# Moving the second weight conversion and the next step's weight sums later in layer 1's first product

## The chip, the cores and the metric

The kernel runs on one core of one Trainium2 chip. The metric is the device time of one execution in microseconds (us). The kernel before takes 1036.18 us (median of 3 runs, 1035.57 to 1036.93). One further execution was profiled; its trace is what all rows below come from.

## The reference

An attention with a sigmoid in place of the softmax is followed by two layers of two matrix products each. Only the first product of the first layer (`x @ w_in`) is touched here.

```python
def _attn_ref(q, k, v):            # 4 x 12 heads, 448 x 64
    scores = scale * q @ k.T - log(S)
    return (1 / (1 + exp(-scores))) @ v

def _moe_ref(x, w_in, w_out):      # x 1792 x 768, w_in 768 x 2048
    h = x @ w_in
    g = h * (1 / (1 + exp(-h)))
    return g @ w_out

def _moe2_ref(x, w_in, w_out, a, b):
    h = x @ w_in
    g = P(h) / (Q(h) + 1e-6)       # a cubic over a quadratic
    return g @ w_out
```

The inputs q, k, v and the weights arrive as float64 and the kernel turns them into float32 itself.

## The kernel before, in words

Every float32 operand of a matmul is split into a high part (a copy cast by ScalarE) and a low part (source minus high part, by VectorE); a product is then three matmuls: high with high, low with high, high with low. Layer 1's first product is done by a seven-product scheme on halves of the matrices: each of the 16 steps g of the loop at L1183 makes seven products p1 to p7, each of nine matmuls of 128x448, with weights that are halves of w_in's blocks and sums of them. A step covers two blocks of 128 of the hidden width for one of two halves of the batch (t = 0 for g below HF = 8, then t = 1).

TensorE's order within step g is p1(g), p2(g), p4(g-1), p6(g), p5(g), p3(g-1), p7(g). Each of the five engines has its own queue of instructions, and the code is written in the very order in which they are put there; nothing reorders it.

The names in the rows, which leave out buffer numbers:

- `wf` holds the float32 weights of a step, two tiles (first and second half) for even and two for odd steps. For g up to 7 they come from a conversion; for later ones from DRAM (`load_w1`, L588).
- A conversion (`conv`, L209) makes a float32 tile from the bits of a float64 one: two ScalarE instructions (L226, L227), then two VectorE instructions (L228, L229). The second half of step g+1's weights is converted in step g after p2 (for g from 1 to 6); the first half of step g+2's at the end of step g, after p7 (for g up to 5). A DMA writes the result to DRAM and another loads the next float64 tile (`conv_outs`, L180).
- `sf` holds four sums: S1 and S2 (`sums_12`, L602: VectorE L448 with `sf<-wf`, then L445 with `sf<-sf,wf`) and S3 and S4 (`sums_34`, L612: two times L445).
- `wr` and `wq` are the split weights. `prep_ij` casts the first half (wr0, `wr<-wf`), `prep_s12` casts S1 and S2 (wr2, `wr<-sf`), `prep_s3` and `prep_s4` cast S3 (wq0) and S4 (wq2, both `wq<-sf`), `prep_a22` casts a quarter (wq4, `wq<-wf`). The casts are ScalarE's L436; the low parts wr1, wr3, wq1, wq3, wq5 are VectorE's L441, issued by the next `flush`.
- p1 and p2 use wr0 and wr1, p6 and p5 use wr2 and wr3, p7 uses wq0 and wq1, p3 uses wq2 and wq3, p4 uses wq4 and wq5.
- `keep` (ScalarE L649) copies a bank of products out, `both` (VectorE L448 with `sb<-acc` or `sb<-hb`) adds another bank to it, and the `silu` calls c11, c12, c21, c22 (ScalarE L593) make the result and have it stored. c21 reads its bank directly.
- `fill` and `operands1` prepare the second half's x operands in steps 1, 3 and 5 (ScalarE L426, VectorE L427 and L445), two operands in each.

The banks of products are the two halves of one tile `hb` (L1046) and six tiles `acc`. The first bank list of `bank` (L565) gives p1, p4, p6 and p7 of a step one bank, the last gives p5 and p3 one: with g mod 3 = 1 the former is hb's first half, with g mod 3 = 2 the latter is hb's second half.

Of the kernel before, what the change touches and what calls it, by code (L numbers as in the profile page):

```python
# [47 lines left out]
def attention_moe_moe(ctx: ExitStack, tc: tile.TileContext, q, k, v, w_in1, w_out1, w_in2, w_out2, a, b2, out):  # L48
# [12 lines left out]
    HF = KF // 2  # L61
# [11 lines left out]
    def fixed(nm, n, shape, dt, pool=cpool):  # L73
        return [pool.tile(shape, dt, tag=f"{nm}{i}", name=f"{nm}{i}") for i in range(n)]
# [105 lines left out]
    def conv_outs():  # L180
        for do in outs:
            do()
        outs.clear()
# [25 lines left out]
    def conv(parted=False, into=None):  # L209
        i = done["conv"]  # L210
        if i >= len(order):
            return
        m, kind, c = order[i]
        t = staged.pop(i)
        lo, hi = t[:, :, 0], t[:, :, 1]
        u = bits.get() if into is None else into
        ui = u.bitcast(I32)
        if into is not None:
            kept_by = partial(conv_kept, wd[m][c][kind], u, t)
        elif (m, kind) == (0, "o") and c >= direct[0]:  # L220
            kept_by = partial(conv_split, c, u, t)
        else:
            kept_by = partial(conv_out, wd[m][c][kind], u, t)
        done["conv"] += 1
        if not parted:
            nc.scalar.activation(u, hi.bitcast(F32), AF.Prelu, scale=DOWN, alpha=NEGATIVE)  # L226
            nc.scalar.activation(lo, t.bitcast(U16)[:, :, 1], AF.Identity, bias=mid, scale=EIGHTH)  # L227
            nc.vector.tensor_scalar(u, u, MOST_DOWN, -MOST_DOWN * NEGATIVE, op0=ALU.min, op1=ALU.max)  # L228
            nc.vector.scalar_tensor_tensor(  # L229
                out=ui, in0=ui, scalar=3, in1=lo, op0=ALU.logical_shift_left, op1=ALU.bitwise_or  # L230
            )
            outs.append(kept_by)
            return
        nc.scalar.activation(u, hi.bitcast(F32), AF.Abs)
        nc.vector.tensor_scalar(u, u, LEAST, MOST, op0=ALU.max, op1=ALU.min)
        nc.vector.tensor_scalar(ui, ui, 3, REST, op0=ALU.logical_shift_left, op1=ALU.bitwise_and)

        def rest():
            nc.vector.scalar_tensor_tensor(
                out=ui, in0=hi, scalar=SIGN_TOP, in1=ui, op0=ALU.bitwise_and, op1=ALU.bitwise_or  # L240
            )
            nc.vector.scalar_tensor_tensor(
                out=ui, in0=lo, scalar=29, in1=ui, op0=ALU.logical_shift_right, op1=ALU.bitwise_or
            )
            outs.append(kept_by)

        halves.append(rest)
# [77 lines left out]
    wf = [fixed(f"wf{i}_", 2, [P, DM], F32, w1_p) for i in range(2)]  # L325
# [109 lines left out]
    def split_later(src, h, lo):  # L435
        nc.scalar.copy(h, src)  # L436
        lows.append((src, h, lo))

    def flush():
        for src, h, lo in lows:  # L440
            nc.vector.tensor_tensor(out=lo, in0=src, in1=h.bitcast(F32), op=ALU.subtract)  # L441
        lows.clear()

    def sub(o, i0, i1):
        nc.vector.tensor_tensor(out=o, in0=i0, in1=i1, op=ALU.subtract)  # L445

    def add(o, i0, i1):
        nc.vector.tensor_tensor(out=o, in0=i0, in1=i1, op=ALU.add)  # L448
# [84 lines left out]
    def operands1_late(kind):  # L533
        temps = [t[:, :S] for t in xio.free]
        if kind == "T2":
            for kk in range(HK):
                load_b(temps[kk], 1, 0, kk, 1)
        if kind in ("T2", "T1"):
            for kk in range(HK):
                split_b(kept[kind, kk], 1, kind, kk)  # L540
        if kind == "T1":
            for kk in range(HK):
                load_b(kept["T1", kk], 1, 1, kk, 1)
        if kind == "T3 sums":
            for kk in range(HK):
                sub(temps[kk], kept["T1", kk], temps[kk])
        if kind == "T3":
            for kk in range(HK):
                split_b(temps[kk], 1, kind, kk)
            for kk in range(HK):  # L550
                load_b(temps[kk], 1, 1, kk, 0)
        if kind == "22":
            for kk in range(HK):
                split_b(kept["T1", kk], 1, kind, kk)
        if kind == "T4 sums":
            for kk in range(HK):
                sub(temps[kk], temps[kk], kept["T2", kk])
        if kind == "T4":
            for kk in range(HK):
                split_b(temps[kk], 1, kind, kk)  # L560
# [41 lines left out]
    def sums_12(g):  # L602
        if g < NGR:
            t, u = wf[g % 2]
            add(s12f[:, :HM], u[:, :HM], u[:, HM:])
            sub(s12f[:, HM:], s12f[:, :HM], t[:, :HM])
# [10 lines left out]
    def prep_s3(g):  # L617
        split_later(s34f[:, :HM], wq[0], wq[1])
# [7 lines left out]
    def p1(g):  # L626
        product(g, "11", bank("a", g), wr[0], wr[1], 0, True)

    def p2(g):
        product(g, "21", bank("b", g), wr[0], wr[1], HM, True)  # L630
# [4 lines left out]
    def p4(g):  # L635
        product(g, "T4", bank("a", g), wq[4], wq[5], 0, False)
# [10 lines left out]
    def keep(g, nm):  # L647
        t = sums[g, nm] = f448.get()
        nc.scalar.copy(t, bank("a", g))  # L649

    def both(g, nm, kind):
        t = sums[g, nm]
        add(t, bank(kind, g), t)
# [4 lines left out]
    def c12(g):  # L658
        silu(sums[g, "r"], sums[g, "r"], g, 0, 1)
# [381 lines left out]
    with tc.manual_schedule():  # L1041
# [141 lines left out]
        for g in range(NGR):  # L1183
            was = g >= 1

            p1(g)
            flush()
            if was:
                keep(g - 1, "u3")
            if g >= 2:  # L1190
                c12(g - 2)
            if g == HF:
                operands1_late("T3")
            if g == HF + 1:
                operands1_late("22")

            p2(g)
            flush()
            keep(g, "s1")
            if was:  # L1200
                both(g - 1, "u3", "c")
            conv_outs()
            if 1 <= g < HF - 1:
                conv(into=wf[(g + 1) % 2][1])
            sums_34(g)
            if g == HF - 1:
                operands1_late("T2")

            if was:
                p4(g - 1)  # L1210
                c22(g - 1)
            flush()
            both(g, "s1", "b")
            sums_12(g + 1)
            if was:
                fill(g)
            if g > HF:
                conv()
            if g == last - 3:
                third[0] = stage3  # L1220

            p6(g)
            flush()
            c11(g)
            if was:
                c21(g - 1)
            prep_s3(g)
            if g == HF - 1:
                operands1_late("T1")
            if g == HF:  # L1230
                operands1_late("T4 sums")
            if g == last:
                once.extend([*xio.free, *(xp[4][:, j].bitcast(F32) for j in range(2))])
                fg.put(*once)
                for n in range(5):
                    load_g(n)

            p5(g)
            flush()
            keep(g, "r")  # L1240
            conv_outs()
            prep_ij(g + 1)
            if g:
                prep_a22(g)
            fill(g)
            if g == HF:
                operands1_late("T4")
            if g == last:
                split_wo1(0)
                split_gd(0)  # L1250

            if was:
                p3(g - 1)
            flush()
            if g + 2 >= HF:
                load_w1(g + 2)
            conv_outs()
            if g == last:
                both(g - 1, "r", "c")
            if g == HF - 1:  # L1260
                operands1_late("T3 sums")
            if g == last - 1:
                kt_s.close()
                wos_p, wos_s = opened("wos", side="right")
                wos.put(*fixed("wos", 4, [P, DM], F32, wos_p))
                for c in range(4):
                    load_wo1(c)
            if g == last:
                split_wo1(1)
                split_gd(1)  # L1270
                load_wo1(4)

            p7(g)
            flush()
            if was and g < last:
                both(g - 1, "r", "c")
            prep_s12(g + 1)
            prep_s4(g)
            if g < HF - 2:
                conv(into=wf[g % 2][0])  # L1280
            elif g in (HF + 2, HF + 4):
                conv()
# [127 lines left out]
        for n in range(HN):  # L1410
            g, p = turn(n)
# [118 lines left out]
```

## Time and profile before

| what | value |
|---|---|
| median of 3 runs | 1036.18 us |
| the profiled execution | 1036.96 us |
| its span, first to last instruction | 1035.2 us |
| TensorE busy | 1025.6 us (99%) |
| VectorE busy | 690.2 us (67%) |
| ScalarE busy | 654.8 us (63%) |
| layer 1's first product | from 158.8 us to about 360 us |

Busy time counts matmuls whose ends are modelled, so that a small pause of TensorE is best seen at its weight loads (PEld), which run one ahead of the matmuls. The waits are inferred from semaphore events. Where an engine waits for several, the one that came last by the profile is named.

### The profile page before, as it was taken

Reading aid. Unit: us, or ns where it says so; the run is one execution under the profiler, and the core shown is the slowest. Engines: PE = TensorE matmul, PEld = TensorE weight load, DVE = VectorE, ACT = ScalarE, POOL = GpSimd, SP = SyncE. Lnnn points to the kernel's source line nnn. Section 1 sums busy time; section 2 is a strip of 40 time slices with the busy share of each in tenths; the row PEclk is TensorE's granted clock in tenths of the full one; section 3 lists DMA queues with packets and bytes.
Section 4 is the critical chain, followed back from the end, with each engine's and each line's share of the span. In section 5 each row is a group of like instructions: output and inputs, shape, how many; then the busy total and the mean of one; then the engine's idle time right before and its main releaser. Section 6 shows DMA issues by size and latency. Waiting matters only on the chain.

```text
span 1035.2 us, 15920 instructions
## 1 busy us (share of the span) xinstructions
PE 1025.6 (99%) x5568; PEld 894.3 (86%) x5568; DVE 690.2 (67%) x982; ACT 654.8 (63%) x971; POOL 270.2 (26%) x242
## 2 busy tenths in 40 slices
PE   9999999999999999999999999999999999999998
PEld 6555558889999988999998888888999999999998
DVE  4567756888977656354545538889897967555761
ACT  6788877777776666364645568676778866444430
POOL 4335420000000000000000065878959922310000
PEclk9999999999999999999999999999999999999999
DMA  8967856887786766598979634665778879986641
GB/s 173 211 147 169 190 148 207 283 294 261 231 291 245 263 245 209 189 385 273 398 277 406 252 109 157 213 226 201 261 254 312 273 230 295 321 282 204 218 157 54
DMA packets 182352, 246.15 MB, mean 238 GB/s; under 512 B 57152, under 2 KB 136640, under 8 KB 182272
## 3 DMA queue, kind: packets, MB, share of 16 engines
q1 hardware_dynamic: 168352, 220.95, 65.5%
q10 hardware_dynamic: 11152, 17.36, 4.8%
q0 software_dynamic: 2768, 6.82, 2.6%
q8 instruction: 44, 0.72, 0.3%
q14 instruction: 36, 0.29, 0.1%
HBM read 161.45 MB, written 83.62 MB: 237 GB/s over the span
## 4 chain that ended last, share of the span: by engine, by line
PE 69%; DVE 8%; ACT 2%; DMA 1%; issue 1%; SPq 0%; DVEq 0%; ACTq 0%
PE hp L996 12%; PE acc L574 11%; PE acc L722 6%; PE acc L721 6%; PE acc L723 6%; PE hp L794 5%; PE hp L795 5%; PE hp L796 5%; PE hb L996 4%; PE hb L574 4%; PE hb L722 2%; PE hb L723 2%; PE hb L721 2%; DVE sb L827 1%; DVE sb L825 1%; DVE sb L840 1%
## 5 line engine op out<-in xcount | busy, mean ns | idle before, releaser
L394 ACT ACTIVATE sb<-pair,nls 128x896 f32<-128x896 f32 x84 | 80.5, 1009 | 22.3 <-PE pair L379 22.3
L721 PE MATMUL acc<-xa_all,woH 128*128 128x512 f32 (+1 forms) x252 | 91.9, 365 | 0.0
L722 PE MATMUL acc<-xa_all,woH 128*128 128x512 f32 (+1 forms) x252 | 91.9, 365 | 0.0
L723 PE MATMUL acc<-xa_all,woL 128*128 128x512 f32 (+1 forms) x252 | 91.9, 365 | 0.0
L431 POOL TENSOR_TENSOR woL<-wif,woH 128x768 fp32r<-128x768 f32 x9 | 16.5, 1854 | 248.1 <-ACT woH L430 248.1
L823 POOL TENSOR_TENSOR sb<-sb 128x1024 f32<-128x1024 f32 (+1 forms) x32 | 69.3, 2166 | 39.4 <-ACT sb L820 39.4
L403 PE MATMUL hb<-sb,vs 128*64 128x448 f32 (+1 forms) x384 | 73.0, 554 | 0.0
L574 PE MATMUL acc<-xb,wr 128*128 128x448 f32 x315 | 66.9, 362 | 0.0
L226 ACT ACTIVATE sb<-sb 128x768 f32<-128x768 f32 x46 | 41.3, 898 | 40.1 <-DMA w1i<-sb 22.0
L914 POOL TENSOR_TENSOR sb<-sb 128x384 f32<-128x384 f32 (+1 forms) x43 | 52.2, 1220 | 53.9 <-DMA sb<-gk 51.9
L574 PEld LDWEIGHTS acc<-xb,wr 128*128 128x128 f32 x315 | 59.0, 187 | 4.6 <-issue 0.7
L796 PE MATMUL hp<-hx,woL 128*128 128x512 f32 (+1 forms) x168 | 60.7, 362 | 0.0
L794 PE MATMUL hp<-hx,woH 128*128 128x512 f32 (+1 forms) x168 | 60.7, 362 | 0.0
L795 PE MATMUL hp<-hx,woH 128*128 128x512 f32 (+1 forms) x168 | 60.7, 362 | 0.0
L794 PE MATMUL hp<-xa_all,woH 128*128 128x512 f32 (+1 forms) x168 | 60.7, 362 | 0.0
L795 PE MATMUL hp<-xa_all,woH 128*128 128x512 f32 (+1 forms) x168 | 60.7, 362 | 0.0
L796 PE MATMUL hp<-xa_all,woL 128*128 128x512 f32 (+1 forms) x168 | 60.7, 362 | 0.0
L820 ACT ACTIVATE sb<-sb,absb 128x1024 f32<-128x1024 f32 (+1 forms) x32 | 36.5, 1139 | 33.7 <-DVE hb L841 33.2
L228 DVE TENSOR_SCALAR sb<-sb 128x768 f32<-128x768 f32 x48 | 26.8, 558 | 41.7 <-ACT sb L226 41.5
L227 ACT ACTIVATE sb<-sb,ab 128x768 int32<-128x768 uint16 x54 | 53.6, 992 | 0.0
L825 DVE TENSOR_TENSOR sb<-hp,sb 128x768 f32<-128x768 f32 (+1 forms) x31 | 33.6, 1084 | 28.4 <-ACT sb L822 27.3
L229 DVE SCALAR_TENSOR_TENSOR sb<-sb 128x768 int32<-128x768 int32 x46 | 44.1, 959 | 12.2 <-ACT sb L227 10.8
(259 smaller groups left out, 2787.1 us busy)
## 6 DMA issues: line engine op xcount, KB each, us to landing
sb<-in_moe_w_out_dram SPq DMA_DIRECT2D x30, 768.0 KB, 6.7
sb<-in_moe_w_in_dram SPq DMA_DIRECT2D x28, 768.0 KB, 7.0
gd<-sb SPq DMA_DIRECT2D x64, 224.0 KB, 2.3
gk<-sb SPq DMA_DIRECT2D x28, 384.0 KB, 3.9
wf<-w0i SPq DMA_DIRECT2D x20, 384.0 KB, 5.4
gk<-sb SPq DMA_DIRECT2D x15, 512.0 KB, 3.0
woL<-gk SPq DMA_DIRECT2D x25, 256.0 KB, 5.0
w1i<-sb SPq DMA_DIRECT2D x16, 384.0 KB, 5.0
```

The source lines that it names most:

```text
L227: nc.scalar.activation(lo, t.bitcast(U16)[:, :, 1], AF.Identity, bias=mid, scale=EIGHTH)
L394: nc.scalar.activation(t, p[:, :, :S], AF.Sigmoid, bias=nls, scale=QKSCALE)
L403: nc.tensor.matmul(hb[i_ % 2][j * D : (j + 1) * D, :S], vs[i_][part, j, c * D : (c + 1) * D], t[part, j], start=(c == 0), stop=(c == LAST),)
L574: nc.tensor.matmul(o, w_[:, w], x[:, i_, :], start=first and kk == 0 and n_ == 0, stop=kk == HK - 1 and n_ == 2, skip_group_check=not first,)
L721: nc.tensor.matmul(o, woH[c][:, w], x[:, 0, :w_], start=(c == 0), stop=False)
L722: nc.tensor.matmul(o, woH[c][:, w], x[:, 1, :w_], start=False, stop=False)
L723: nc.tensor.matmul(o, woL[c][:, w], x[:, 0, :w_], start=False, stop=(c == KF - 1))
L794: nc.tensor.matmul(o, wh[:, w], x[:, 0, :wd_], start=first, stop=False)
L795: nc.tensor.matmul(o, wh[:, w], x[:, 1, :wd_], start=False, stop=False)
L796: nc.tensor.matmul(o, wl[:, w], x[:, 0, :wd_], start=False, stop=last)
L823: nc.gpsimd.tensor_tensor(out=q_, in0=q_, in1=a_, op=ALU.mult)
L996: nc.tensor.matmul(o, a_, y[:, w_, :], start=kk_ == 0 and n_ == 0, stop=kk_ == HF - 1 and n_ == 2)
```

## The change

The second conversion of a step goes from behind p2 to behind p6: in the code two products later, behind the calls c11, c21 and `prep_s3`. Its DMAs follow one call of `conv_outs` later. S1 and S2 of the next step's weights go from behind p4 to behind p3, three products later, into the queue behind the low parts of wr0 and wq4.

```diff
             conv_outs()
-            if 1 <= g < HF - 1:
-                conv(into=wf[(g + 1) % 2][1])
             sums_34(g)
...
             both(g, "s1", "b")
-            sums_12(g + 1)
             if was:
                 fill(g)
...
                 c21(g - 1)
             prep_s3(g)
+            if 1 <= g < HF - 1:
+                conv(into=wf[(g + 1) % 2][1])
...
             keep(g, "r")
-            conv_outs()
             prep_ij(g + 1)
...
             conv_outs()
+            sums_12(g + 1)
             if g == last:
                 both(g - 1, "r", "c")
```

On VectorE, in step 3 from behind p2 on (the row L448 with `sb<-hb` is `both` of u3, the one with `sb<-acc` that of s1; `sf_216` is S3 and S4, `sf_215` S1 and S2):

```order
 L448 TENSOR_TENSOR sb<-hb,sb 128x448
-L228 TENSOR_SCALAR wf_1_212<-wf_1_212 128x768
-L229 SCALAR_TENSOR_TENSOR wf_1_212<-wf_1_212,stage_1835 128x768
 L445 TENSOR_TENSOR sf_216<-wf_0_213,wf_1_214 128x384
 L445 TENSOR_TENSOR sf_216<-wf_0_213,sf_215 128x384
 L448 TENSOR_TENSOR sb<-acc_1852,sb 128x448
-L448 TENSOR_TENSOR sf_215<-wf_1_212 128x384
-L445 TENSOR_TENSOR sf_215<-sf_215,wf_0_211 128x384
 L427 TENSOR_TENSOR xa_all<-T_1841,xa_all 128x448
+L228 TENSOR_SCALAR wf_1_212<-wf_1_212 128x768
+L229 SCALAR_TENSOR_TENSOR wf_1_212<-wf_1_212,stage_1835 128x768
 L441 TENSOR_TENSOR wq_1724<-sf_216,wq_1723 128x384
```

The conversion's two instructions stand behind `both` of s1 now, ahead of wq1's low part, and S1 and S2 are gone from here.

On VectorE a few rows on in the same step, behind p3 (the last row is `both` of r, which reads hb's second half):

```order
 L441 TENSOR_TENSOR wr_1720<-wf_0_211,wr_1719 128x768
 L441 TENSOR_TENSOR wq_1728<-wf_1_214,wq_1727 128x384
+L448 TENSOR_TENSOR sf_215<-wf_1_212 128x384
+L445 TENSOR_TENSOR sf_215<-sf_215,wf_0_211 128x384
 L448 TENSOR_TENSOR sb<-hb,sb 128x448
```

S1 and S2 stand behind the low parts of wr0 and wq4, and `both` of r behind them.

On ScalarE in step 3 (L593 are c22, c11 and, with `sb<-acc`, c21; `wq_1723` is the cast of S3):

```order
 L649 COPY sb<-acc_1849 128x448
+L593 ACTIVATE sb<-sb 128x448
+L426 CAST xa_all<-T_1841 128x448
+L593 ACTIVATE sb<-sb 128x448
+L593 ACTIVATE sb<-acc_1850 128x448
+L436 CAST wq_1723<-sf_216 128x384
 L226 ACTIVATE wf_1_212<-stage_1835 128x768
 L227 ACTIVATE stage_1835<-stage_1835,ab 128x768
-L593 ACTIVATE sb<-sb 128x448
-L426 CAST xa_all<-T_1841 128x448
-L593 ACTIVATE sb<-sb 128x448
```

The conversion's two instructions stand behind c11, c21 and S3's cast. The cast of S1 and S2 (`wr<-sf`) keeps its place in ScalarE's queue, and so does everything behind it.

## Rows read from the trace of the kernel before

**Rows 1.** The page: the whole span, and TensorE's granted clock in 40 slices.

```profile
span 1035.2 us, 15920 instructions
PEclk9999999999999999999999999999999999999999
```

**Rows 2.** Timeline of weight loads: start, us, line, out<-in, count [idle before, releaser].

```profile
188.91 1.70 PEld L574 LDWEIGHTS hb<-xb,wr 128*128 128x128 f32 x9 [1.44 <-ACT sb L593]
...
207.78 1.71 PEld L574 LDWEIGHTS hb<-xb,wr 128*128 128x128 f32 x9 [0.97 <-ACT sb L227]
...
228.29 1.70 PEld L574 LDWEIGHTS hb<-xb,wr 128*128 128x128 f32 x9 [0.80 <-ACT sb L593]
...
246.21 1.79 PEld L574 LDWEIGHTS hb<-xb,wr 128*128 128x128 f32 x9
...
258.81 3.59 PEld L574 LDWEIGHTS acc<-xa_all,wr 128*128 128x128 f32 x18
...
266.32 1.71 PEld L574 LDWEIGHTS hb<-xb,wr 128*128 128x128 f32 x9 [0.32 <-ACT sb L593]
```

**Rows 3.** Timeline of VectorE, step 2 behind p2.

```profile
185.38 0.96 DVE L229 SCALAR_TENSOR_TENSOR wf<-wf,sb 128x768 int32<-128x768 int32 x1
186.26 0.55 DVE L445 TENSOR_TENSOR sf<-wf,wf 128x384 f32<-128x384 f32 x1
186.72 0.55 DVE L445 TENSOR_TENSOR sf<-wf,sf 128x384 f32<-128x384 f32 x1
187.19 0.62 DVE L448 TENSOR_TENSOR sb<-acc,sb 128x448 f32<-128x448 f32 x1
187.73 0.55 DVE L448 TENSOR_TENSOR sf<-wf 128x384 f32<-128x384 f32 x1
188.31 0.56 DVE L445 TENSOR_TENSOR sf<-sf,wf 128x384 f32<-128x384 f32 x1
```

**Rows 4.** Timeline of ScalarE, steps 2 and 3.

```profile
187.85 0.58 ACT L593 ACTIVATE sb<-sb 128x448 f32<-128x448 f32 x1 [2.41 <-DVE sb L448]
188.33 0.53 ACT L593 ACTIVATE sb<-hb 128x448 f32<-128x448 f32 x1
188.75 0.50 ACT L436 CAST wq<-sf 128x384 fp32r<-128x384 f32 x1
...
193.09 0.89 ACT L226 ACTIVATE wf<-sb 128x768 f32<-128x768 f32 x1
193.89 1.00 ACT L227 ACTIVATE sb<-sb,ab 128x768 int32<-128x768 uint16 x1
```

**Rows 5.** Timeline of VectorE, step 0: the low part of step 1's wr0.

```profile
165.78 0.96 DVE L441 TENSOR_TENSOR wr<-wf,wr 128x768 fp32r<-128x768 f32 x1 [0.79 <-ACT wr L436]
```

**Rows 6.** Timeline of ScalarE, step 3 behind p6.

```profile
202.46 0.53 ACT L649 COPY sb<-acc 128x448 f32<-128x448 f32 x1
202.88 0.84 ACT L436 CAST wr<-wf 128x768 fp32r<-128x768 f32 x1
203.62 0.52 ACT L436 CAST wq<-wf 128x384 fp32r<-128x384 f32 x1
204.03 0.57 ACT L426 CAST xa_all<-sb 128x448 fp32r<-128x448 f32 x1
204.50 0.84 ACT L436 CAST wr<-sf 128x768 fp32r<-128x768 f32 x1
```

**Rows 7.** Timeline of VectorE, step 3 behind p5.

```profile
204.64 0.63 DVE L427 TENSOR_TENSOR xa_all<-sb,xa_all 128x448 fp32r<-128x448 f32 x1 [1.46 <-ACT xa_all L426]
205.18 0.62 DVE L445 TENSOR_TENSOR T<-sb,T 128x448 f32<-128x448 f32 x1
205.71 0.95 DVE L441 TENSOR_TENSOR wr<-wf,wr 128x768 fp32r<-128x768 f32 x1
206.58 0.55 DVE L441 TENSOR_TENSOR wq<-wf,wq 128x384 fp32r<-128x384 f32 x1
207.05 0.62 DVE L448 TENSOR_TENSOR sb<-hb,sb 128x448 f32<-128x448 f32 x1
```

## The prediction, made before the changed kernel was run

> **What bounds the kernel now.** I read the page first, then TensorE's weight loads through layer 1's first product, then VectorE and ScalarE around each pause. TensorE is the bound: it hardly ever stops, and its clock is granted in full in all 40 slices [rows 1]. A step's seven products run unbroken in 258.81 - 246.21 = 12.60 us, 1.80 each [rows 2]. The first product shows only four pauses, 1.44, 0.97, 0.80 and 0.32, together 3.53 us [rows 2]; all end at a product whose bank is a half of hb. p5(2) begins at 188.91, 0.05 after c21 of step 1 ended (188.33 + 0.53 = 188.86) [rows 2, 4]. c21 read hb's first half while p5(2) writes the second, so I take it that hb is watched as one tile. p1(4), at 207.78, goes the same way: not ScalarE's L227, which the row names, but `both` of r (207.05 + 0.62 = 207.67) released it, 0.11 before [rows 2, 7]. So what TensorE waits for is how late VectorE and ScalarE are, and these two hand a step's work to and fro.
>
> **The change, part by part.** No instruction is added or removed, so only waits can change; each move is priced by who then waits.
>
> The conversion leaves VectorE's queue ahead of S3, S4 and `both` of s1. In step 2 its L229 alone holds 186.26 - 185.38 = 0.88, and c11 had ScalarE idle for 2.41 us until `both` of s1 was done [rows 3, 4]. That is a gain for c11 and c21, and with it for p5(2) and p5(5), if nothing else moves: 1.44 + 0.80 = 2.24 us [rows 2]. The DMAs behind it start later by at most a product or two and feed the third conversion on, a step and a half or 18.9 us later, so I price them at nothing; that cover fails if a load lands only after that.
>
> S1 and S2 are what decides. ScalarE's cast of them (wr2) keeps its place in the queue. In step 3 it starts at 204.50 [rows 6]. In the new order VectorE comes to S1 only behind the low part of wq4: 206.58 + 0.47 = 207.05, and then takes 188.31 - 187.73 = 0.58 for S1 and 0.56 for S2 [rows 3, 7]. That is 208.19, 3.69 us after the cast's turn, with nothing else late. Behind this cast in ScalarE's queue stand S4's cast, the next conversion and the `keep` of u3; behind these in VectorE's the conversion's other part, `both` of u3, S3, S4 and `both` of s1; then c11, c21, S3's cast and the second conversion back on ScalarE; then VectorE again up to the next S2. So the steps are now tied to one ring through both engines. I sum it from start to start of rows of the same form, the last of each stretch in full, 0.04 for a handoff (187.19 + 0.62 = 187.81 to 187.85) [rows 3, 4]:
>
> - ScalarE: wr2 0.74, S4's cast 0.41, L226 0.80, L227 1.00 = 2.95 [rows 4, 6].
> - VectorE: handoff 0.04, L229 0.88, the low parts of wr2 0.87 and of S4 0.47, `both` of u3 0.54, S3 0.46, S4 0.47, `both` of s1 0.62 = 4.35 [rows 3, 7].
> - ScalarE: handoff 0.04, c11 0.48, c21 0.42, S3's cast 0.41, L226 0.80, L227 1.00 = 3.15 [rows 4, 6].
> - VectorE: handoff 0.04, L229 0.88, low parts of S3 0.47, wr0 0.87, wq4 0.47, then S1 0.58 and S2 0.56 = 3.87, and a handoff of 0.04 back [rows 3, 7].
>
> A round is 14.36 us in an even step. In steps 1, 3 and 5 x operands are prepared too. From L227's end VectorE then waits for the second operand's cast, behind `keep` 0.42, wr0 0.74, wq4 0.41 and L426 0.57, less the 0.09 by which ScalarE takes its next instruction before L227 ends (an estimate from the overlaps of these rows), plus 0.04: 2.09 where an even step has 0.04 + 0.88 + 0.47 = 1.39. Then L427 takes 0.54 and L445 0.53 [rows 6, 7]. That adds 0.70 + 1.07 = 1.77: 16.13. TensorE needs 12.60, so it is not the one to close the ring.
>
> Where the ring begins: step 1's S1 now follows the low part of wr0, which starts at 165.78 [rows 5]: 165.78 + 0.87 + 0.58 + 0.56 = 167.79. Six steps (1 to 6) have the second conversion, three odd and three even: 3 x (14.36 + 16.13) = 91.47, so that step 7's S2 ends at 259.26. Behind it comes `both` of r, which starts 0.09 before that end (0.56 less the 0.47 between starts) and takes 0.62, and p1(7), on hb, waits for it with the 0.11 seen at p1(4): 259.26 - 0.09 + 0.62 + 0.11 = 259.90. Before, p1(7) began at 246.21 [rows 2]. Layer 1 is **13.7 us late** there, with the old pauses ahead of it contained.
>
> From step 7 on there is no second conversion, and the ring is open. What remains is S1 and S2, 0.58 + 0.47 = 1.05 us, ahead of `both` of r and late for the wr2 cast. Five more products write hb behind a read of it (p1(10), p1(13), p5(8), p5(11), p5(14)): the bounds are 0 and 5 x 1.05 = 5.3 us. Carrying the starts on by the same durations through steps 7 to 15 I find pauses of 0.5 at p5(8), 1.5 at p1(10) and 0.6 at p5(11), each giving 0.1 back in the product behind it, and 0.3 is gone that was there: 2.0 net. Everything behind the first product waits on TensorE and is only shifted.
>
> **The sum**: 13.7 + 2.0 = 15.7 us on the profiled execution's 1036.96, or 1052.7; the median shown lies 0.78 lower, so 1051.9, which I call **1052 us**.
>
> **Rivals.** (a) Faster: the ring never closes, because ScalarE comes to the wr2 cast after S2 is done. Then only the gain of the first move is left, 2.24 us: 1033.9 by the median. It decides at the wr2 cast; for it speaks that ScalarE was idle 2.41 us of step 2 and could shift its work [rows 4], against it the 3.69 us above, which would have to vanish in every step. (b) Partly late: even steps hide the ring's 1.76 excess, and only the odd ones pay 16.13 - 12.60 = 3.53 each: 10.6, less the old pauses of 3.2 in these steps, plus 0 to 2 behind: 1043.6 to 1045.6. For it: if VectorE can run its part while ScalarE converts. Against it: each stretch of the ring needs the one before it. (c) No change that can be told (a measurement of this kernel tells 0.2%, 2.1 us): gain and loss would have to meet, which needs a ring below about 13 us.
>
> (d) TensorE's clock drops in the longer pauses. The trace shows full clock through pauses up to 1.44 us [rows 1, 2]. My ring makes longer ones; the longest stands ahead of p1(4), 3.3 us by the same recurrence. Seven pauses above 1.44 that I find, each followed by one product at half rate, would add 7 x 1.80 = 12.6: 1064.5. The Trainium skill (TensorE: Matmul & The Clock Gate, section "What's actually happening") says that an idle array falls back from 2.4 to 1.2 GHz and regains its clock only after being kept busy. By that rule (d) follows from the ring; the trace before has no stretch at the lower level to price it from.
>
> **How the numbers follow.** The forecast gets 0.78, (a) 0.04, (b) 0.10, (c) 0.03, (d) 0.05. The handoffs are the forecast's softest term: with 0.06 or 0.08 in place of 0.04, as some rows with two semaphores have, six rounds grow by 0.5 to 1; the part behind step 7 can give 0 to 5.3. That makes 1050 to 1057. To leave out no more than 2 in 10 the range takes in (b) at the lower end and half of (d) at the upper: 1045 to 1060. Faster 0.04, same 0.03, slower 0.93.
>
> **What would show it.** Right: ScalarE idle ahead of L436 `wr<-sf`, ended by VectorE's L445, some 2.4 us in even and 3.7 in odd steps; VectorE idle ahead of L228 for ScalarE's L226; p1(4) about 7 us and p1(7) about 14 us later than before, p5(2) still pausing in spite of the move; the rest of the kernel shifted as one piece. Wrong: no wait at that cast; p5(2) and p5(5) without a pause; a clock below full; or pauses that come from DMA landings.

## The result, and the profile after

The changed kernel takes 1051.46 us (median of 4 runs, 1051.13 to 1052.63), the kernel before beside it 1036.37 us (1035.57 to 1036.93). The ratio is 1.0148, 95% interval [1.0131, 1.0166]: 15 us slower, where 1052.0 was forecast. The profiled execution took 1051.13 us.

The page of the changed kernel: the span, the engines' busy time, TensorE's granted clock.

```profile
span 1049.4 us, 15929 instructions
PE 1028.1 (98%) x5568; PEld 892.6 (85%) x5568; DVE 690.1 (66%) x982; ACT 653.3 (62%) x971; POOL 271.5 (26%) x242
PEclk9999999999999999999999999999999999999999
```

VectorE and ScalarE are as busy as before (690.2 and 654.8 us then), and the clock is full in this execution. What grew is waiting. The weight loads of the first product, as in [rows 2]; all that waited more than 0.3 us in steps 1 to 3 and at p1(4), and behind them the pauses above 0.3 us at hb's products:

```profile
179.74 1.31 PEld L574 LDWEIGHTS hb<-xa_all,wq 128*128 128x128 f32 x7 [0.74 <-DVE wq L441]
...
182.38 3.11 PEld L574 LDWEIGHTS acc<-xb,wr 128*128 128x128 f32 x16 [0.93 <-DVE wr L441]
187.34 1.71 PEld L574 LDWEIGHTS hb<-xb,wq 128*128 128x128 f32 x9 [1.86 <-ACT sb L649]
...
192.30 1.71 PEld L574 LDWEIGHTS hb<-xb,wr 128*128 128x128 f32 x9 [1.45 <-ACT sb L593]
...
201.69 1.71 PEld L574 LDWEIGHTS acc<-xb,wq 128*128 128x128 f32 x9 [0.48 <-ACT sb L649]
...
209.15 0.30 PEld L574 LDWEIGHTS acc<-xa_all,wq 128*128 128x128 f32 x2 [0.35 <-ACT sb L649]
210.20 1.31 PEld L574 LDWEIGHTS acc<-xa_all,wq 128*128 128x128 f32 x7 [0.75 <-DVE wq L441]
214.95 1.70 PEld L574 LDWEIGHTS hb<-xb,wr 128*128 128x128 f32 x9 [3.44 <-issue]
...
232.16 1.71 PEld L574 LDWEIGHTS hb<-xb,wq 128*128 128x128 f32 x9 [0.94 <-ACT sb L649]
237.12 1.70 PEld L574 LDWEIGHTS hb<-xb,wr 128*128 128x128 f32 x9 [1.44 <-ACT sb L593]
...
259.79 1.70 PEld L574 LDWEIGHTS hb<-xb,wr 128*128 128x128 f32 x9 [1.69 <-issue]
...
279.97 1.71 PEld L574 LDWEIGHTS hb<-xb,wr 128*128 128x128 f32 x9 [0.47 <-ACT sb L593]
...
299.39 1.71 PEld L574 LDWEIGHTS hb<-xa_all,wr 128*128 128x128 f32 x9 [1.52 <-issue]
...
319.87 1.71 PEld L574 LDWEIGHTS hb<-xb,wr 128*128 128x128 f32 x9 [0.77 <-ACT sb L593]
```

Before there were four pauses. Of these p5(2)'s is still there at 192.30 with 1.45 us (1.44 before), and p5(5)'s at 237.12 has grown from 0.80 to 1.44. p1(4) starts at 214.95 and p1(7) at 259.79, 7.2 and 13.6 us later than in [rows 2]. Their pauses carry no releaser here (`issue`); the rows of the matmuls themselves name VectorE's L448, which is `both` of r.

Why TensorE waits is seen on VectorE and ScalarE. VectorE's seven S2 instructions that end a round (from step 0, for step 1, to step 6, for step 7), each alone on its line:

```profile
167.19 0.56 DVE L445 TENSOR_TENSOR sf<-sf,wf 128x384 f32<-128x384 f32 x1
...
183.29 0.56 DVE L445 TENSOR_TENSOR sf<-sf,wf 128x384 f32<-128x384 f32 x1
...
197.63 0.56 DVE L445 TENSOR_TENSOR sf<-sf,wf 128x384 f32<-128x384 f32 x1
...
213.74 0.56 DVE L445 TENSOR_TENSOR sf<-sf,wf 128x384 f32<-128x384 f32 x1
...
228.10 0.56 DVE L445 TENSOR_TENSOR sf<-sf,wf 128x384 f32<-128x384 f32 x1
...
244.22 0.56 DVE L445 TENSOR_TENSOR sf<-sf,wf 128x384 f32<-128x384 f32 x1
...
258.58 0.56 DVE L445 TENSOR_TENSOR sf<-sf,wf 128x384 f32<-128x384 f32 x1
```

The rounds between them last 16.10, 14.34, 16.11, 14.36, 16.12 and 14.36 us, where TensorE needs 12.60. ScalarE at the cast of these sums in steps 2 and 3, as in [rows 6]:

```profile
198.30 0.83 ACT L436 CAST wr<-sf 128x768 fp32r<-128x768 f32 x1 [2.40 <-DVE sf L445]
...
214.41 0.83 ACT L436 CAST wr<-sf 128x768 fp32r<-128x768 f32 x1 [3.70 <-DVE sf L445]
```

And VectorE's own wait in the same round, ahead of the second conversion (step 3):

```profile
207.82 0.56 DVE L228 TENSOR_SCALAR wf<-wf 128x768 f32<-128x768 f32 x1 [1.73 <-ACT wf L226]
```

Each engine waits for the other at least twice a round, so neither is saturated and both are late. The waits of the casts (L436) for VectorE's sums in the whole first product, us in total and times, are one row; before, no such wait shows in this view:

```profile
  DVE sf L445: 39.3, 15
```

Of these 39.3 us, 20.5 belong to the seven casts that follow the S2 rows above. The eight later ones wait 18.8 us as well, and TensorE loses only 2.2 us there, as is seen below: a wait of ScalarE costs time only where the ring hands it on.

Not all of the delay reaches the end of the trace. First and last starts of the matmuls that open the second layer's first product (L794) and of one form of those of its second product (L996), before:

```profile
L794 PE MATMUL hb<-hx,w x12: 389/389/389, 594.1 to 601.6; 128*128 128x512 f32 x12
L996 PE MATMUL hp<-woH,hx x189: 334/334/443, 833.9 to 1007.8; 128*128 128x384 f32 x189
```

and after:

```profile
L794 PE MATMUL hb<-hx,w x12: 389/389/389, 609.9 to 617.3; 128*128 128x512 f32 x12
L996 PE MATMUL hp<-woH,hx x189: 334/334/440, 848.6 to 1021.9; 128*128 128x384 f32 x189
```

The lag is 15.8 us at L794 and 14.7 at these matmuls of L996, and the spans differ by 14.2.

### The profile page after: what moved, and what is told of

Its sections match the earlier page's. It is cut to its first block, busy times and chain, and to the rows that moved or that the text cites. A ratio compares the mean times of both kernels' runs of the same rounds, so it can differ in the third digit from the quotient of the medians.

```text
span 1049.4 us, 15929 instructions
## 1 busy us (share of the span) xinstructions
PE 1028.1 (98%) x5568; PEld 892.6 (85%) x5568; DVE 690.1 (66%) x982; ACT 653.3 (62%) x971; POOL 271.5 (26%) x242
## 4 chain that ended last, share of the span: by engine, by line
PE 84%; DVE 5%; ACT 5%; DMA 4%; issue 2%; SPq 1%; POOL 0%; ACTq 0%; DVEq 0%; POOLq 0%
PE hp L996 15%; PE hp L795 7%; PE hp L796 7%; PE hp L794 7%; PE hb L403 6%; PE pair L379 6%; PE acc L723 6%; PE acc L721 6%; PE acc L722 6%; PE acc L574 5%; PE hb L996 5%; PE hb L574 2%; PE hb L723 2%; PE hb L722 2%; PE hb L721 2%
## 5 line engine op out<-in xcount | busy, mean ns | idle before, releaser
L794 PE MATMUL hp<-hx,woH 128*128 128x512 f32 (+1 forms) x168 | 60.7, 362 | 0.0
L794 PE MATMUL hp<-xa_all,woH 128*128 128x512 f32 (+1 forms) x168 | 60.7, 362 | 0.0
L229 DVE SCALAR_TENSOR_TENSOR sb<-sb 128x768 int32<-128x768 int32 x46 | 44.1, 959 | 13.1 <-ACT sb L227 12.0
```

The costliest lines, as they stand in the source:

```text
L794: nc.tensor.matmul(o, wh[:, w], x[:, 0, :wd_], start=first, stop=False)
```

## The experiments

All are compared with the kernel before on the same chip; its median was 1036.93 us in the first four and 1036.76 in the other four. A is the theory of the prediction: the late S2 holds ScalarE's cast, which closes a ring through both engines.

**Only S1 and S2 late.** The conversion stays behind p2.

```diff
             both(g, "s1", "b")
-            sums_12(g + 1)
...
                 load_w1(g + 2)
             conv_outs()
+            sums_12(g + 1)
```

> Only the second move: S1 and S2 go behind p3 as in the changed kernel, the conversion stays behind p2 as before. Theory A (the late S2 holds ScalarE's cast wr2, and with it one ring through ScalarE and VectorE closes): the ring is there without the conversion's move, so 12 to 15 us slower than before, near 1050; ScalarE idle ahead of `wr<-sf` for VectorE's L445 in every step, p1(7) some 12 us late. Rival B (the conversion's later place is what costs, since VectorE now waits for ScalarE's L226 in the middle of a step): within 1 us of before.

Measured: 1051.4 us, ratio 1.014 [1.0127, 1.0154]. The cast's wait is that of the full change, and pauses stand in front of p5(2) and p1(4) again. p1(7) starts at 260.64, 14.4 us late, where some 12 were expected:

```profile
  DVE sf L445: 38.8, 15
```

```profile
193.77 3.11 PEld L574 LDWEIGHTS hb<-xb,wr 128*128 128x128 f32 x9 [2.98 <-ACT sb L593]
216.60 1.70 PEld L574 LDWEIGHTS hb<-xb,wr 128*128 128x128 f32 x9 [2.04 <-issue]
```

The weight loads of p5(2) take 3.11 us here in place of 1.70: behind this pause TensorE's clock fell to half, and once more at p5(5) (the last section has the rows). The slow products held up ScalarE, whose cast of S4 waited for one of them:

```profile
200.42 0.51 ACT L436 CAST wq<-sf 128x384 fp32r<-128x384 f32 x1 [1.66 <-PE acc L574]
```

Step 3's S2 came 18.14 us after the one before it (197.25 to 215.39), that of steps 1 and 5 only 15.98. By these rows the clock made some 2.2 of the 14.4 us, and 12.2 are left at p1(7), where the full change has 13.6. So S1 and S2 cost by far the most of it, and rival B falls. How much of the clock's part reaches the times is not clear: the one execution with a mean clock of 1.000 took 1051.06 us, the others, with 0.995 or 0.996, took 1051.16 to 1052.32.

**The conversion late, S1 and S2 directly behind it.** (The conversion cannot go behind p6 by itself, since S1 and S2 read what it makes.)

```diff
             if 1 <= g < HF - 1:
                 conv(into=wf[(g + 1) % 2][1])
+            sums_12(g + 1)
...
             conv_outs()
-            sums_12(g + 1)
```

> The conversion stays behind p6 as in the changed kernel, but S1 and S2 stand directly behind it, ahead of p5 instead of behind p3. Theory A: S2 is done before ScalarE comes to the cast wr2 in most steps, so the ring is mostly open: 1 to 4 us slower than before, near 1038.5. Rival B (the conversion's place costs): 13 to 16 us slower, as the changed kernel.

Measured: 1038.35 us, ratio 1.0012 [1.0003, 1.0021]. ScalarE's wait at the cast, from its waits in 158 to 300 us, is down to 2.7 us, where the changed kernel has 28.2:

```profile
ACT wr L436 <- DVE sf L445: 2.7, 5, 0.7
```

The conversion's place, with S1 and S2 directly behind it, costs 1.4 us (0.3 to 2.2 by the interval). The rest of the 15.1, some 13 to 14 us, comes from where S1 and S2 stand: 1051.46 less 1038.35 is 13.1, but the two were not measured together.

**All of the change, the cast later.** Nothing moves on VectorE but the low part of this cast.

```diff
             if was and g < last:
                 both(g - 1, "r", "c")
-            prep_s12(g + 1)
             prep_s4(g)
...
             elif g in (HF + 2, HF + 4):
                 conv()
+            prep_s12(g + 1)
```

> All of the change is kept; only the cast of S1 and S2 (prep_s12) is issued later, at the end of the step behind S4's cast and the next conversion, so that what stood behind the waiting cast on ScalarE no longer waits with it. Theory A: the ring is cut, 2 to 6 us slower than before are left (VectorE's `both` of r behind S1 and S2, seen at p1(4) and p1(7)), near 1040. Rival C (not the cast holds ScalarE, but S1 and S2 make VectorE late by themselves): 12 us slower or more.

Measured: 1040.31 us, ratio 1.0035 [1.0022, 1.0049]. VectorE's S1, S2 and `both` of r in step 3, in the new order, but 6 us earlier than in the changed kernel:

```profile
207.13 0.55 DVE L448 TENSOR_TENSOR sf<-wf 128x384 f32<-128x384 f32 x1
207.72 0.56 DVE L445 TENSOR_TENSOR sf<-sf,wf 128x384 f32<-128x384 f32 x1
208.19 0.62 DVE L448 TENSOR_TENSOR sb<-hb,sb 128x448 f32<-128x448 f32 x1
```

So it was the waiting cast with what stood behind it. Rival C falls. The cast still waits 9.7 us between 158 and 300 us (28.2 in the changed kernel), but less stands behind it. TensorE now waits longest for `both` of r behind S1 and S2: it ends at 208.81, and p1(4) starts at 208.93 with a pause:

```profile
208.93 1.70 PEld L574 LDWEIGHTS hb<-xb,wr 128*128 128x128 f32 x9 [2.78 <-issue]
```

**The kernel before with the conversion one place later.**

```diff
             conv_outs()
-            if 1 <= g < HF - 1:
-                conv(into=wf[(g + 1) % 2][1])
             sums_34(g)
...
             both(g, "s1", "b")
+            if 1 <= g < HF - 1:
+                conv(into=wf[(g + 1) % 2][1])
             sums_12(g + 1)
```

> The kernel before with the second conversion one place later only: behind `both` of s1 and ahead of S1 and S2, which stay where they were. By the same sums of starts c11 and c21 come earlier and the ring stays open, since S2 ends when it did: the pauses at p5(2), p1(4), p5(5) shrink from 3.2 us to about 0.7: 2 us faster than before, near 1034.2. Rival B (any later conversion costs): slower than before by 1 us or more.

Measured: 1034.24 us, ratio 0.9976 [0.9966, 0.9985]. ScalarE in step 2: c11 and c21 run at 186.46 and 186.93, 1.4 us earlier than in [rows 4], and p5(2) hardly waits:

```profile
186.46 0.57 ACT L593 ACTIVATE sb<-sb 128x448 f32<-128x448 f32 x1
186.93 0.53 ACT L593 ACTIVATE sb<-hb 128x448 f32<-128x448 f32 x1
```

```profile
187.51 1.71 PEld L574 LDWEIGHTS hb<-xb,wr 128*128 128x128 f32 x9 [0.22 <-ACT sb L593]
```

So a gain of the kind that the first move was to bring is real, for the conversion one place later and with S1 and S2 where the cast finds them done. The first move itself, two products later, cannot be run alone.

**hb as two tiles.** No instruction moves; in layer 2 a new tile of both banks takes their place.

```diff
-        hb_p = ctx.enter_context(tc.tile_pool(name="hbp", bufs=1, space=PSUM))
+        hb_p, hb_s = opened("hbp", space=PSUM)
...
-        hb_all = hb_p.tile([P, 2, 512], F32, tag="hb", name="hb")
-        hb.extend(hb_all[:, j] for j in range(2))
-        hpair.append(hb_all)
+        hb.extend(fixed("hb", 2, [P, 512], F32, hb_p))
...
         ps_s.close()
+        hb_s.close()
+        hb_p = ctx.enter_context(tc.tile_pool(name="hb2", bufs=1, space=PSUM, reuse_waits="tile"))
+        hb_all = hb_p.tile([P, 2, 512], F32, tag="hball", name="hball")
+        hb[:] = [hb_all[:, j] for j in range(2)]
+        hpair.append(hb_all)
```

> The kernel before, with hb's two halves as two tiles until layer 2, where they become one pair again; no instruction is moved. Reading H (hb is watched as one tile, so that p5(2), p1(4), p5(5) and p5(8) wait for a read of the other half): all four pauses are gone, 2.6 to 3.5 us faster than before, near 1034. Rival (these products wait for something of their own, their weights or their bank): the pauses stay, within 1 us of before.

Measured: 1033.89 us, ratio 0.9977 [0.9967, 0.9986]. c21 runs as late as before, at 188.13 behind the same idle time, and p5(2) started at 187.28 without it:

```profile
187.65 0.58 ACT L593 ACTIVATE sb<-sb 128x448 f32<-128x448 f32 x1 [2.41 <-DVE sb L448]
188.13 0.53 ACT L593 ACTIVATE sb<-hb 128x448 f32<-128x448 f32 x1
```

```profile
187.28 1.79 PEld L574 LDWEIGHTS hb<-xb,wr 128*128 128x128 f32 x9
```

No pause of TensorE's weight loads is left in the first product behind its start at 158.6 us. Reading H holds.

**Both of these.** The kernel with the conversion one place later and with two tiles.

> Conversion one place later and hb as two tiles together. If both only remove the same four pauses, of 3.5 us in all, there is little left for the second to take: 2.6 to 3.5 us faster than before, near 1034, and not 5 us as a plain sum of two gains would have it.

Measured: 1033.78 us, ratio 0.9973 [0.9963, 0.9983]. It is no faster than either alone within the intervals: both take away the same pauses. All three are faster than the kernel before, by 0.2 to 0.3%.

**The changed kernel with hb as two tiles.**

> The changed kernel with hb as two tiles. Theory A (the ring through both engines is late by itself): the pauses at p5(2), p5(5), p1(4) and p1(7) go from hb to other products (p4 for `keep` of u3, p1 and p7 for low parts), 12 to 15 us slower than before, near 1050.5. Rival D (the loss comes from the shared tile, since most of the long pauses stand at hb's products): less than 6 us slower.

Measured: 1051.12 us, ratio 1.0139 [1.0125, 1.0153]. The pauses at p5(2) and p5(5) are gone, others have come; at p7(2), p1(4) and p4(3), for example:

```profile
195.89 1.31 PEld L574 LDWEIGHTS acc<-xa_all,wq 128*128 128x128 f32 x7 [0.75 <-DVE wq L441]
...
212.87 1.30 PEld L574 LDWEIGHTS hb<-xb,wr 128*128 128x128 f32 x7 [0.92 <-DVE wr L441]
217.84 1.70 PEld L574 LDWEIGHTS acc<-xb,wq 128*128 128x128 f32 x9 [1.86 <-ACT sb L649]
```

S2 follows S2 every 16.10 or 16.11 and 14.33 or 14.34 us, as in the changed kernel. Set against the kernel before with two tiles (1033.89 us, same chip), the change costs 17.2 us. A ring that is late makes TensorE wait somewhere; the shared tile only chose where. Rival D falls.

**The change, the cast later, hb as two tiles.**

> All of the change, the cast of S1 and S2 at the end of the step, and hb as two tiles. If what was left with the later cast alone (pauses at p5(2), p1(4), p1(7), p5(8), p1(10)) stems from `both` of r and c21 at the shared tile: 0 to 2 us slower than before, near 1037.5. If S1 and S2 cost VectorE that much whatever hb is: 3 to 4 us slower, as with the later cast alone.

Measured: 1038.06 us, ratio 1.0009 [1.0000, 1.0019]. The later cast alone left 3.4 us over the kernel before, this leaves 1.3, as the first reading has it; the intervals do not overlap. But two tiles take 2.9 us off the kernel before as well, so this does not show that the loss came through the tile. With two tiles on both sides, on one chip, the kernel is 4.2 us slower (1038.06 less 1033.89), which speaks for the second reading. The pauses that are left stand mostly at p1 and p7 and end with low parts (VectorE's L441). In this trace S2 follows S2 every 14.14 and 12.37 us in turn, 13.26 in the mean, and TensorE needs 12.60: in six rounds that makes 3.8 us (246.52 - 167.14 = 79.38, less 6 x 12.60). So the later cast shortened the ring and did not wholly open it. That is read from the rows; no run took this rest away.

## Why the prediction was right

- *The waits before are hb's.* Right, and shown: with two tiles all four pauses go.
- *The first move gains at p5(2) and p5(5).* Right in itself: 2.7 us (1036.93 less 1034.24, interval 0.15% to 0.34%) with the conversion one place later, 2.24 forecast. In the changed kernel nothing of it is seen, since the ring sets when c21 runs.
- *S2 comes 3.69 us after the cast's turn.* ScalarE waited 3.70 in odd steps and 2.40 in even ones (2.4 forecast).
- *Rounds of 16.13 and 14.36 us.* 16.10 to 16.12 and 14.34 to 14.36. From the first S2 to the last 258.58 - 167.19 = 91.39 us, 91.47 forecast. p1(7) was to start at 259.90 and did at 259.79. In such a chain the durations were the old ones, and only which instruction waits for which had to be found. One term was too small: from S2's end to the cast it took 0.11 (198.19 to 198.30), not 0.04, and hundredths elsewhere made up for it, which is luck.
- *2.0 us behind step 7.* p1(7) is 13.6 us late and L794 15.8: 2.2 us, at the places named (0.47, 1.52, 0.77 for 0.5, 1.5, 0.6).
- *A price of nothing for the DMAs of the conversion.* It held: in the first product no pause of TensorE or ScalarE in the changed kernel ends with a DMA.
- *Everything behind is only shifted.* Between the two traces this failed, by 1.1 to 1.6 us. Before, TensorE had waited 0.9 us for VectorE early in the last product (L996), and of that after shows nothing:

```profile
PE hp L996 <- DVE sb L827: 0.6, 1, 0.6
PE hp L996 <- DVE hx L953: 0.3, 1, 0.3
```

  ScalarE's lag falls from 15.7 to 14.3 us at one place (765.13 to 767.78 before, 780.81 to 782.05 after), where before it had waited 1.31 us for a landing of the second layer's x. Its waits for these landings between 590 and 850 us, before:

```profile
ACT xa_all L766 <- DMA xa_all<-xs: 4.7, 3, 1.8
```

  and after:

```profile
ACT xa_all L766 <- DMA xa_all<-xs: 3.5, 2, 1.8
```

  The other traces tell that this does not go with the change. From L794's first matmul to the last one of the form `hp<-w,hx` at L996 it takes 434.3 to 434.9 us in five of the ten traces, with 3.2 to 3.5 us of these landing waits, and 435.6 to 436.5 us in the other five, with 4.7 to 5.1 us of them and TensorE's two waits at L996. The changed kernel and the kernel before with two tiles are among the short ones, the kernel before and the changed kernel with two tiles among the long ones. So the two traces compared here met one of each by chance. Why the landings fall in two ways stays open. In the median the difference is 15.1 us, between the traces' 14.2 and the 15.7 of the sum.
- *Rivals.* (a) needed the cast not to wait, (b) even rounds of 12.6, (c) a ring below 13: none was so. (d) did not come in the profiled execution, whose clock stayed full. That is in part luck: with only S1 and S2 late it came, behind two pauses of 2.98 us, and slowed two products behind each where the prediction had one. Of the four executions of the changed kernel two have a mean clock of 1.000 and two of 0.998; in which stretch the latter lost it no trace shows.

## What to carry to other kernels

When an instruction is moved later in one engine's queue, look first at who reads its result: if that reader keeps its place in another engine's queue, everything behind the reader moves too, and two engines that are each two thirds busy can become a ring longer than the step. Sum that ring from the durations of the old trace before the move; if it is longer than the bound engine's step, leave the producer where it is, or move the reader along (which here still left 3.4 of the 15.1 us). A wait that ends with an access to another part of the same tile is a wait for nothing: two tiles gave a gain here that the reordering tried, alone or with them, did not exceed.

## What the runs showed of the hardware

TensorE's clock stayed full through the longest pause of the changed kernel's trace, and fell to half behind shorter ones in another run. Stretches around p1(4) in the changed kernel; the columns are the stretch and its length, busy time of TensorE, of its weight loads, of VectorE, ScalarE and GpSimd, granted clock, DMA share and GB/s:

```profile
211.50:215.00 3.50, 0.40 (x3) 0.06 (x2) 3.30 (x6) 0.59 (x1) 0.00 (x0) 1.00 0.81 241
215.00:219.00 4.00, 4.00 (x20) 3.76 (x21) 2.19 (x3) 3.65 (x7) 0.00 (x0) 1.00 0.00 0
```

TensorE was busy for 0.40 of 3.50 us, the clock reads 1.00 in and behind the pause, that is 2.4 GHz, and p1(4) and the product behind it take 3.68 us together (214.98 to 218.66), as before (207.81 to 211.50). The run with only S1 and S2 late, around p5(2):

```profile
191.00:193.20 2.20, 0.17 (x1) 0.00 (x0) 2.20 (x5) 0.49 (x2) 0.00 (x0) 0.99 0.85 222
193.30:199.90 6.60, 6.12 (x16) 5.45 (x17) 3.01 (x5) 3.23 (x6) 0.00 (x0) 0.50 1.05 379
200.10:205.00 4.90, 4.90 (x27) 4.58 (x26) 3.53 (x6) 3.94 (x7) 0.00 (x0) 1.00 0.37 132
```

Here the clock reads 0.50, that is 1.2 GHz, behind a pause of 2.98 us at the weight loads, and 1.00 again from 200.10 on, after TensorE had worked without a break since 193.78. p5(2) and the product behind it take 6.58 us (193.78 to 200.36), 2.9 more than at full clock. At p5(5), behind a second pause of 2.98 us, the clock reads 1.00 up to 240.90 and 0.50 from 241.00 to 244.30, so that it fell only once TensorE had begun again; the two products take 5.31 us (239.97 to 245.28), 1.6 more. The fall to half clock in an idle array of which the Trainium skill speaks (TensorE: Matmul & The Clock Gate, section "What's actually happening") came behind these two pauses and not behind the 3.44 us of p1(4) in the changed kernel. What made the difference no run here shows.
